# Threshold attention and Fourier mixing on one core: the last 64 queries' scores in four 64x64 tiles of TensorE

## Chip, core and metric

The kernel runs on one core of one Trainium2 chip. The metric is the device time of one execution in microseconds (us). TensorE (PE in the profile) multiplies, VectorE (DVE), ScalarE (ACT) and GpSimd (POOL) work on vectors, and SyncE (SP) issues most of the transfers.

## What is computed

An attention with a threshold, whose output is the input of a block that mixes with a Fourier transform and then applies two dense layers. All of it is fp32.

```python
# q, k, v: (8 batches, 8 heads, 576 positions, 64)
scores = matmul(q, k.T) / 8
thresh = max(scores, axis=-1) - tau               # tau = 0.02
scores = where(scores >= thresh, scores, -1e9)
attn = exp(scores - max(scores)); attn /= sum(attn) + 1e-9
x = matmul(attn, v)            # heads side by side: (8, 576, 512)
mixed = real(fft(fft(x, axis=1), axis=2))
u = x + mixed
un = (u - mean(u)) / sqrt(var(u) + 1e-6)          # over the 512 columns
out = u + maximum(un @ w_ch1, 0) @ w_ch2          # w_ch1: 512x2048, w_ch2: 2048x512
```

## The kernel before, in words

**Pairs and steps.** The attention goes through 32 pairs of heads (8 batches, 4 pairs each), and each pair takes 5 steps, t = 0 to 4, so there are 160 steps i = 5 n + t. A pair's two heads j = 0, 1 lie on the partition halves 0 to 63 and 64 to 127, since a head has 64 columns. Steps 0 to 3 take 128 queries of both heads each: 2 x 128 rows of 576 scores. Step 4 takes the last 64 queries of both heads, which together fill 128 rows.

**Preparation of a pair.** `prep_pair` (L401, in step 3 of the pair before) turns the loaded k and q with VectorE's transposes into kT and qT (L408, L409, L411). kT has 640 columns: the lower half needs the keys in natural order, the upper half has its last 64 keys also in front, so that both heads' last 64 keys end up in the middle of the two rows of weights. `prep_ends` (L416, in step 1) copies on GpSimd the last 64 queries of each head into q_ends, a 128x128 tile whose off-diagonal blocks are zero (L420). `load_v` (L143) loads v of the next pair with two transfers a head: 512 rows and the last 64, whose tile has zeros on the other half.

**Scores** (`scores`, L427). In steps 0 to 3 four matmuls of 64 rows by 128 columns, 288 keys each, one for each half of the keys (c) and head (j), write two PSUM tiles "sc" (L440). In step 4 two matmuls with all 128 rows (L446) multiply the block-diagonal q_ends by kT: each row of the result is one query of one head, with all its 576 scores, in one "sc" tile. There are two "sc" buffers: steps 0 to 3 use both, step 4 uses one.

**Softmax.** VectorE takes the negated maximum of each row (L461 or L520), ScalarE the exponentials (L469, L526) and the threshold (L473, L530), VectorE masks and sums in one instruction (L477, L540), adds 1e-9 and inverts (`inverse`, L385, L388). In the first two batches (steps 0 to 39) `softmax` (L452) does it in one go, and the inverse is spread over columns (`spread_inverse`, L501, L509) and applied later to the values. From the third batch on it comes in three parts with other work between them (`softmax_first`, `_second`, `_third`, L514 to L555), and ScalarE scales the weights themselves (L549). In step 4 there is one row block, so each of these has one instruction, and the last 64 weights are copied next to the others (L504, L554).

**Weights and values.** `weights_in_parts` (L561) transposes the weights of step i - 1 with TensorE: one transpose of the 128 columns that hold both heads' last 64 keys (pe, L587), in the first two batches one of the spread inverse (L590), and four for each head's other 512 keys (pw, L605); step 4 has one pe and four pw. ScalarE copies them out (L593, L597 for step 4's ends; L607, L609). `values_in_parts` (L614) multiplies by v, the two heads in the two column halves of TensorE (L636), and the product waits for ScalarE's copies. PSUM tiles "mm" (pe, pw, pv and the dense layers' ph and po) share four buffers.

**What sets the order.** The program is written out by hand (`manual_schedule`): each engine works through its instructions in the order in which the Python code issues them, and waits only for data and buffers. In the first batch `step` (L1509) issues, for every step, scores, softmax, a column mean of the weights (L360) or filler matmuls (`busy`, L104 to L111) and the transposes of the step before; pieces of the conversion of the dense layers' weights (L296 to L319) go between. In the first batch the scores are sorted by head (L436). The second batch has `second_batch` (L1657); from the third batch on the loop of L1749 puts pieces of the dense layers (L1210, L1400, taken by `fill`, L1489, by a budget of columns) between the parts of the softmax. SyncE's queue carries q, k, v, the dense layers' weights (w<-f, some 1 MB each, issued two loads ahead) and the outputs.

Of the kernel before, what the change touches and what calls it, by code (L numbers as in the profile page):

```python
# [9 lines left out]
FP32 = mybir.dt.float32  # L10
INT32 = mybir.dt.int32
UINT32 = mybir.dt.uint32
ALU = mybir.AluOpType
# [34 lines left out]
def kernel(  # L48
# [94 lines left out]
    def load_v(n):  # L143

        b, p = n // NPAIR, PAIRS[n % NPAIR]
        vt = v_in[n % 2]
        for j in range(2):
            h = 2 * p + (j + p) % 2
            nc.sync.dma_start(
                out=vt[:, j:8:2, :], in_=v[b, h, 0:512, :].rearrange("(t p) d -> p t d", p=128)  # L150
            )
            nc.sync.dma_start(out=vt[64 * j : 64 * j + 64, 8 + j, :], in_=v[b, h, 512:576, :])
# [15 lines left out]


    q_ends = const.tile([128, 128], FP32, name="q_ends")  # L170
    nc.gpsimd.memset(q_ends[:, :], 0.0)
# [211 lines left out]
    def inverse(i, nh):  # L383
        den = sb.tile([128, 2], FP32, tag="den", bufs=3, name="den")
        nc.vector.tensor_reduce(  # L385
            out=den[:, 0:nh], in_=den_eps[i % 3][:, 0:nh, :], axis=AXIS_X, op=ALU.add
        )
        nc.vector.reciprocal(den[:, 0:nh], den[:, 0:nh])  # L388
        return den

    heads = {}
    steps = {}
    xs = {}
# [7 lines left out]
    def prep_pair(n):  # L401

        q_raw, k_raw = loaded.pop(n)
        kT = sb.tile([128, D + S], FP32, tag="kT", name="kT")
        nc.vector.transpose(kT[:, D : D + S], k_raw[:, :])  # L408
        nc.vector.transpose(kT[64:128, 0:D], k_raw[64:128, 512:S])  # L409
        qT = sb.tile([128, S], FP32, tag="qT", bufs=1, name="qT")  # L410
        nc.vector.transpose(qT[:, :], q_raw[:, :])  # L411
        heads[n] = (qT, kT, v_in[n % 2])
        if n + 1 < B * NPAIR and not late:
            load_pair(n + 1)

    def prep_ends(n):  # L416

        for j in range(2):
            hp = slice(64 * j, 64 * j + 64)
            nc.gpsimd.tensor_copy(q_ends[hp, hp], heads[n][0][hp, 512:S])  # L420
# [6 lines left out]
    def scores(i):  # L427
        n, t = divmod(i, NT)
        qT, kT = heads[n][0:2]

        nh = 2 if t < 4 else 1
        sc = [ps.tile([128, 2, 512], FP32, tag="sc", name=f"sc{j}") for j in range(nh)]
        if t < 4:
            order = [(c, j) for c in range(2) for j in range(2)]
            if i < per_batch:
                order.sort(key=lambda cj: cj[1])  # L436
            for c, j in order:
                if True:
                    hp, k0 = slice(64 * j, 64 * j + 64), D * (1 - j)
                    nc.tensor.matmul(  # L440
                        sc[j][:, c, 0:HALF], qT[hp, 128 * t : 128 * t + 128],
                        kT[hp, k0 + HALF * c : k0 + HALF * (c + 1)], start=True, stop=True,
                    )
        else:
            for c in range(2):
                nc.tensor.matmul(  # L446
                    sc[0][:, c, 0:HALF], q_ends[:, :], kT[:, D + HALF * c : D + HALF * (c + 1)],
                    start=True, stop=True,
                )
        steps[i] = (sc, nh)  # L450

    def softmax(i, between=None, meanwhile=None, behind=None):  # L452


        t = i % NT
        sc, nh = steps[i]
        neg = sb.tile([128, 2], FP32, tag="neg", bufs=3, name="neg")
        thr = sb.tile([128, 2], FP32, tag="thr", bufs=3, name="thr")
        e = sb.tile([128, 2 * S], FP32, tag="e", name="e")
        for j in range(nh):  # L460
            nc.vector.tensor_reduce(  # L461
                out=neg[:, j : j + 1], in_=sc[j][:, :, 0:HALF], axis=AXIS_XY, op=ALU.max,
                negate=True,
            )
        if meanwhile is not None:
            meanwhile()
        for j in range(nh):
            ej = e[:, S * j : S * (j + 1)].rearrange("p (c n) -> p c n", c=2)
            nc.scalar.activation(  # L469
                out=ej, in_=sc[j][:, :, 0:HALF], func=ACT.Exp, bias=neg[:, j : j + 1], scale=1.0  # L470
            )
            if j == 0:
                nc.scalar.activation(  # L473
                    out=thr[:, 0:nh], in_=neg[:, 0:nh], func=ACT.Identity,
                    bias=thr_off[:, :], scale=-1.0,
                )
            nc.vector.scalar_tensor_tensor(  # L477
                out=ej, in0=sc[j][:, :, 0:HALF], scalar=thr[:, j : j + 1], in1=ej,
                op0=ALU.is_ge, op1=ALU.mult, accum_out=den_eps[i % 3][:, j, 0:1],
            )  # L480
            if between is not None and j == 0:
                next(between)
        if behind is not None:
            behind()
        den = inverse(i, nh)
        if between is not None:
            for _ in between:
                pass
        if normalized(i // NT):
            nc.vector.tensor_scalar(  # L490
                out=e[:, 0:S], in0=e[:, 0:S], scalar1=den[:, 0:1], scalar2=None, op0=ALU.mult
            )
            if nh == 2:
                nc.scalar.activation(
                    out=e[:, S : 2 * S], in_=e[:, S : 2 * S], func=ACT.Copy, scale=den[:, 1:2]
                )
            steps[i] = (e, None)
        else:
            steps[i] = (e, den[:, 0:nh])

    def spread_inverse(i):  # L501
        e, den = steps[i]
        if i % NT == 4:
            nc.scalar.copy(e[:, S : S + 64], e[:, 512:S])  # L504
        if den is None:
            return
        nh = den.shape[1]
        rec = sb.tile([128, 2 * D], FP32, tag="rec", name="rec")
        nc.scalar.copy(  # L509
            rec[:, :].rearrange("p (j d) -> p j d", j=nh), _repeated(den, 2 * D // nh)  # L510
        )
        steps[i] = (e, rec)

    def softmax_first(i):  # L514
        sc, nh = steps[i]
        neg = sb.tile([128, 2], FP32, tag="neg", bufs=3, name="neg")
        thr = sb.tile([128, 2], FP32, tag="thr", bufs=3, name="thr")
        e = sb.tile([128, 2 * S], FP32, tag="e", name="e")
        for j in range(nh):
            nc.vector.tensor_reduce(  # L520
                out=neg[:, j : j + 1], in_=sc[j][:, :, 0:HALF], axis=AXIS_XY, op=ALU.max,
                negate=True,
            )
        for j in range(nh):
            ej = e[:, S * j : S * (j + 1)].rearrange("p (c n) -> p c n", c=2)
            nc.scalar.activation(  # L526
                out=ej, in_=sc[j][:, :, 0:HALF], func=ACT.Exp, bias=neg[:, j : j + 1], scale=1.0
            )
            if j == 0:
                nc.scalar.activation(  # L530
                    out=thr[:, 0:nh], in_=neg[:, 0:nh], func=ACT.Identity,
                    bias=thr_off[:, :], scale=-1.0,
                )
        steps[i] = (sc, nh, e, thr)

    def softmax_second(i):
        sc, nh, e, thr = steps[i]
        for j in range(nh):
            ej = e[:, S * j : S * (j + 1)].rearrange("p (c n) -> p c n", c=2)
            nc.vector.scalar_tensor_tensor(  # L540
                out=ej, in0=sc[j][:, :, 0:HALF], scalar=thr[:, j : j + 1], in1=ej,
                op0=ALU.is_ge, op1=ALU.mult, accum_out=den_eps[i % 3][:, j, 0:1],
            )
        steps[i] = (nh, e, inverse(i, nh))

    def softmax_third(i):
        nh, e, den = steps[i]
        for j in range(nh):
            nc.scalar.activation(  # L549
                out=e[:, S * j : S * (j + 1)], in_=e[:, S * j : S * (j + 1)], func=ACT.Copy,  # L550
                scale=den[:, j : j + 1],
            )
        if nh == 1:
            nc.scalar.copy(e[:, S : S + 64], e[:, 512:S])  # L554
        steps[i] = (e, None)  # L555
# [5 lines left out]
    def weights_in_parts(i):  # L561
# [25 lines left out]
        nc.tensor.transpose(pe[:, 0, :], e[:, 512:640], ident[:, :])  # L587
# [6 lines left out]
        else:  # L594
            for j in range(2):
                hp = slice(64 * j, 64 * j + 64)
                nc.scalar.copy(ends[hp, 0:kept, q0 : q0 + 64], pe[hp, 0:kept, hp])  # L597
        qs = slice(q0, q0 + (128 if t < 4 else 64))
        for j in range(2 if t < 4 else 1):
# [3 lines left out]
            for c in range(4):  # L603
                c0 = (S + D) * j + 128 * c
# [3 lines left out]
            else:  # L608
                nc.scalar.copy(  # L609
                    e_t[:, :, qs].rearrange("p (j c) q -> p j c q", j=2),  # L610
                    pw[:, :, :].rearrange("p c (j q) -> p j c q", j=2),
# [1298 lines left out]
```

## Time and profile before

| | before |
|---|---|
| median of 3 runs | 1545.87 us (1544.44 to 1548.71) |
| the profiled execution | 1547.94 us |
| its span, first to last instruction | 1546.2 us |
| granted TensorE clock, mean | 0.997 |
| matmul records of TensorE | 9786 |
| step 4 scores (L446) | 128 records of 128x288 columns, 406 ns each |
| steps 0 to 3 scores (L440) | 1024 records of 64 rows, 288 columns, 402 ns or more |

The span is shorter than the execution's time by what lies before the first and after the last instruction. A row of the profile has the line of the kernel, the engine, the operation, out<-in by the program's names and shapes, the number of instructions, and then busy time and mean duration. In the timeline the first two columns are the start and the length of a merged piece, both in us; square brackets tell how long the engine was idle ahead of it and what ended that. A matmul's duration covers its passage through the pipeline, so the cost of one in a row of many is the difference of two starts. Each fp32 matmul leaves two records.

### The profile page before, as it was taken

The page shows a single profiled execution, that of the slowest core. Times are in us where ns is not written, and L with a number is a line of the kernel's source. Part 1 is how long each engine was busy: PE and PEld are TensorE (multiplying, and loading weights), DVE is VectorE, ACT ScalarE, POOL GpSimd, SP SyncE. Part 2 cuts the span into 40 slices and gives each one's busy share as a digit, 9 for nine tenths or more (in the row PEclk, how much of TensorE's full clock was granted, in tenths as well). Part 3 has the DMA queues.
Part 4 walks back from the last instruction along what each step waited for, and adds up shares of the span by engine and source line. Part 5 has one row for each costly group of instructions (what it writes and reads, how often), then busy time and mean ns, then how long its engine had stood idle before and what let it go on. Part 6 is the DMA issues. An engine that isn't in the chain of part 4 may idle for free.

```text
span 1546.2 us, 27021 instructions
## 1 busy us (share of the span) xinstructions
PE 1524.0 (99%) x9786; PEld 1186.0 (77%) x9786; DVE 1063.2 (69%) x2141; ACT 916.4 (59%) x1921; POOL 779.4 (50%) x964
## 2 busy tenths in 40 slices
PE   9999999999999999999999999999999999999999
PEld 5556555556788778887788878887788778989999
DVE  7977676846779466866578566956687657746546
ACT  6875676655666576656775666666665676133131
POOL 3775563034365642546255724554264625647635
PEclk9999999999999999999999999999999999999999
DMA  7423233465956354644455354635464534646655
GB/s 171 130 59 119 78 92 105 139 183 165 280 187 206 92 173 125 186 113 146 146 167 160 120 159 133 199 92 172 120 195 132 160 117 142 220 163 231 234 196 184
DMA packets 248907, 239.31 MB, mean 155 GB/s; under 512 B 197027, under 2 KB 218533, under 8 KB 228678
## 3 DMA queue, kind: packets, MB, share of 16 engines
q1 hardware_dynamic: 246262, 237.28, 50.1%
q8 instruction: 78, 1.28, 0.3%
q10 hardware_dynamic: 2512, 0.30, 0.1%
q14 instruction: 55, 0.45, 0.1%
HBM read 205.93 MB, written 31.46 MB: 154 GB/s over the span
## 4 chain that ended last, share of the span: by engine, by line
PE 91%; DVE 4%; ACT 2%; POOL 1%; DMA 1%; issue 0%; ACTq 0%; DVEq 0%; POOLq 0%
PE ph L1210 25%; PE po L1400 21%; PE pv L636 10%; PE sc L440 10%; PE pw L605 7%; PE po L933 4%; PE ph L909 3%; PE sc L446 2%; PE py L766 2%; PE pe L587 1%; PE pa L783 1%; PE pn L858 1%; PE pa L787 1%; PE pm L360 1%; PE po L1379 1%; DVE neg L461 1%
## 5 line engine op out<-in xcount | busy, mean ns | idle before, releaser
L520 DVE TENSOR_REDUCE neg<-sc 128x1 f32<-128x576 f32 x216 | 154.3, 751 | 117.1 <-PE sc L440 105.5
L526 ACT ACTIVATE e<-sc,neg 128x576 f32<-128x576 f32 x216 | 158.6, 734 | 114.3 <-DVE neg L520 114.3
L1147 DVE TENSOR_TENSOR hs<-ph,hs 128x512 f32<-128x512 f32 (+1 forms) x128 | 105.3, 823 | 167.1 <-PE ph L1210 97.3
L1400 PE MATMUL po<-w,w_all 128*128 128x128 f32 x1728 | 219.4, 276 | 0.0
L1400 PEld LDWEIGHTS po<-w,w_all 128*128 128x128 f32 x1728 | 205.4, 192 | 7.4 <-issue 4.0
L1156 POOL TENSOR_TENSOR w<-hs 128x512 f32<-128x512 f32 x32 | 42.1, 1317 | 312.3 <-ACT hs L1152 249.3
L540 DVE SCALAR_TENSOR_TENSOR e<-sc,thr,e 128x576 f32<-128x576 f32 x216 | 168.4, 812 | 27.2 <-ACT thr L530 27.1
L1210 PE MATMUL ph<-u_t,w 128*128 128x256 f32 x768 | 180.9, 382 | 0.6 <-DMA w<-f 0.6
L607 ACT COPY e_t<-pw 128x512 f32<-128x512 f32 x256 | 148.4, 594 | 44.2 <-PE pw L605 42.7
L440 PE MATMUL sc<-kT,qT 64*128 64x288 f32 x1024 | 168.4, 430 | 5.9 <-DVE e L477 5.5
L605 PE MATMUL pw<-ident,e 128*128 128x128 f32 x1152 | 169.3, 274 | 3.7 <-ACT ends L593 1.9
L549 ACT ACTIVATE e<-e,den 128x576 f32<-128x576 f32 x216 | 157.4, 774 | 2.9 <-DVE den L388 2.2
L1210 PEld LDWEIGHTS ph<-u_t,w 128*128 128x128 f32 x768 | 140.9, 190 | 23.6 <-issue 5.3
L1210 PE MATMUL ph<-w_all,w 128*128 128x256 f32 x672 | 157.1, 382 | 1.1 <-DVE w_all L1132 1.0
L605 PEld LDWEIGHTS pw<-ident,e 128*128 128x128 f32 x1152 | 135.8, 141 | 19.3 <-issue 5.6
L1263 POOL TENSOR_TENSOR w_all<-w_all 128x128 f32<-128x128 f32 (+2 forms) x160 | 121.7, 777 | 44.5 <-DVE w_all L1420 23.4
L1210 PEld LDWEIGHTS ph<-w_all,w 128*128 128x128 f32 x672 | 123.5, 190 | 23.9 <-issue 4.9
L1152 ACT ACTIVATE hs<-hs 128x512 f32<-128x512 f32 (+1 forms) x96 | 74.1, 772 | 113.8 <-DVE hs L1147 113.0
L440 PEld LDWEIGHTS sc<-kT,qT 64*128 64x128 f32 x1024 | 95.1, 186 | 55.4 <-issue 22.9
L1400 PE MATMUL po<-w,hs 128*128 128x128 f32 x912 | 119.8, 278 | 0.0
L1400 PEld LDWEIGHTS po<-w,hs 128*128 128x128 f32 x912 | 109.8, 192 | 9.5 <-issue 8.0
L636 PE MATMUL pv<-e_t,v_in 128*64 128x320 f32 (+1 forms) x512 | 72.1, 423 | 1.5 <-ACT e_t L609 0.8
(227 smaller groups left out, 2910.6 us busy)
## 6 DMA issues: line engine op xcount, KB each, us to landing
w<-f SPq DMA_DIRECT2D x150, 1024.0 KB, 4.9
hs<-in_moe_w_ch_dram SPq DMA_DIRECT2D x23, 512.0 KB, 4.7
q_in<-in_q_dram SPq DMA_DIRECT2D x128, 72.0 KB, 4.1
out_dram<-u SPq DMA_DIRECT2D x36, 256.0 KB, 2.5
k_in<-in_k_dram SPq DMA_DIRECT2D x124, 72.0 KB, 2.4
v_in<-in_v_dram SPq DMA_DIRECT2D x64, 128.0 KB, 5.1
f<-w SPq DMA_DIRECT2D x14, 512.0 KB, 3.3
f<-w SPq DMA_DIRECT2D x7, 1024.0 KB, 4.8
```

The costliest lines, as they stand in the source:

```text
L440: nc.tensor.matmul(sc[j][:, c, 0:HALF], qT[hp, 128 * t : 128 * t + 128], kT[hp, k0 + HALF * c : k0 + HALF * (c + 1)], start=True, stop=True,)
L520: nc.vector.tensor_reduce(out=neg[:, j : j + 1], in_=sc[j][:, :, 0:HALF], axis=AXIS_XY, op=ALU.max, negate=True,)
L526: nc.scalar.activation(out=ej, in_=sc[j][:, :, 0:HALF], func=ACT.Exp, bias=neg[:, j : j + 1], scale=1.0)
L540: nc.vector.scalar_tensor_tensor(out=ej, in0=sc[j][:, :, 0:HALF], scalar=thr[:, j : j + 1], in1=ej, op0=ALU.is_ge, op1=ALU.mult, accum_out ...
L549: nc.scalar.activation(out=e[:, S * j : S * (j + 1)], in_=e[:, S * j : S * (j + 1)], func=ACT.Copy, scale=den[:, j : j + 1],)
L605: nc.tensor.transpose(pw[:, c, :], e[:, c0 : c0 + 128], ident[:, :])
L607: nc.scalar.copy(e_t[:, 4 * j : 4 * j + 4, qs], pw[:, :, :])
L636: nc.tensor.matmul(pv[64 * j : 64 * j + 64, 0:m], vt[:, 2 * c + j, :], e_t[:, 4 * j + c, 0:m] if c < 4 else ends[:, 0, 0:m], start=(c == 0 ...
L1147: nc.vector.tensor_tensor(out=to, in0=bank, in1=to if other is None else other, op=ALU.add)
L1210: nc.tensor.matmul(bank[:, 256 * q : 256 * q + 256].rearrange("p (two n) -> p two n", two=2), left[:, 256 * c + 128 * q : 256 * c + 128 * ...
L1263: return lambda: eng.tensor_tensor(out=to, in0=to, in1=other, op=ALU.add)
L1400: nc.tensor.matmul(to, lefts[m][j][:, s], right_[:, 128 * s : 128 * (s + 1)], start=jn in (0, 4) and s == 0, stop=s == 3, skip_group_check ...
```

## The change

In step 4 the four products (c, j) of half of the keys and one head become four matmuls of 64 rows by 64 columns, 288 keys each, which write one "sc" tile: head j in bank j, half c of the keys on the partition half c. A query's scores are then spread over two partitions, p and p + 64, with 288 each. So:

- q_ends holds the 64 queries of each head on its own partition half, 128x64, and one GpSimd copy fills it for two before.
- The maximum is taken over 288 scores on each partition, the halves are exchanged by two minima over one element (64 partitions each), and a third minimum joins them (`maxima`, `exchange`). The sums are exchanged in the same way ahead of the inverse (den_ends).
- Exponentials, masks and the late scaling have one instruction for each head with 288 columns in place of one with 576. In step 4 `softmax` issues both exponentials ahead of the masks. The copy of the last 64 weights goes.
- The middle 64 keys (256 to 319) take the place of the last 64 as the part that both heads share in one transpose. So kT has another order and 672 columns, made by two transposes of 320 columns and two of 32 on 64 partitions; v is loaded in three transfers a head for two; steps 0 to 3 have matmuls of 256 and 320 keys, in opposite order for the two heads, and their 576 scores lie in a row across the two banks.
- Step 4's ends are copied out in four pieces of 32 partitions in place of two of 64, and in the first two batches its spread inverse in a piece of its own.

The number of matmul instructions rises from 64 to 128 for step 4's scores and stays the same elsewhere; VectorE's instructions rise by 257, ScalarE's by 96, GpSimd's fall by 33, and 64 transfers are added.

```diff
     def load_v(n):
...
-            nc.sync.dma_start(
-                out=vt[:, j:8:2, :], in_=v[b, h, 0:512, :].rearrange("(t p) d -> p t d", p=128)
-            )
-            nc.sync.dma_start(out=vt[64 * j : 64 * j + 64, 8 + j, :], in_=v[b, h, 512:576, :])
+            for first, k0 in ((0, 320), (2, 0)):
+                nc.sync.dma_start(
+                    out=vt[:, first + j : 8 : 4, :],
+                    in_=v[b, h, k0 : k0 + 256, :].rearrange("(t p) d -> p t d", p=128),
+                )
+            nc.sync.dma_start(out=vt[64 * j : 64 * j + 64, 8 + j, :], in_=v[b, h, 256:320, :])
...
-    def inverse(i, nh):
+    def inverse(i):
         den = sb.tile([128, 2], FP32, tag="den", bufs=3, name="den")
...
+        parts = den_eps[i % 3]
+        if i % NT == 4:
+            parts = den_ends
+            exchange(parts[:, :, 2], parts[:, :, 0:1])
+        nc.vector.tensor_reduce(out=den[:, :], in_=parts[:, :, :], axis=AXIS_X, op=ALU.add)
+        nc.vector.reciprocal(den[:, :], den[:, :])
...
-        kT = sb.tile([128, D + S], FP32, tag="kT", name="kT")
-        nc.vector.transpose(kT[:, D : D + S], k_raw[:, :])
-        nc.vector.transpose(kT[64:128, 0:D], k_raw[64:128, 512:S])
+        kT = sb.tile([128, S + 96], FP32, tag="kT", name="kT")
+        nc.vector.transpose(kT[:, 0:320], k_raw[:, 256:S])
+        nc.vector.transpose(kT[:, 352:672], k_raw[:, 0:320])
+        for j, k0 in ((0, 288), (1, 256)):
+            hp = slice(64 * j, 64 * j + 64)
+            nc.vector.transpose(kT[hp, 320:352], k_raw[hp, k0 : k0 + 32])
...
     def prep_ends(n):
...
-        for j in range(2):
-            hp = slice(64 * j, 64 * j + 64)
-            nc.gpsimd.tensor_copy(q_ends[hp, hp], heads[n][0][hp, 512:S])
+        nc.gpsimd.tensor_copy(q_ends[:, :], heads[n][0][:, 512:S])
...
     def scores(i):
...
+        order = [(c, j) for c in range(2) for j in range(2)]
+        if i < per_batch and t < 4:
+            order.sort(key=lambda cj: cj[1])
+        for c, j in order:
+            hp = slice(64 * j, 64 * j + 64)
+            if t < 4:
+                k0, k1 = ((64, 320), (352, 672), (0, 320), (352, 608))[2 * j + c]
+                to = sc[j][:, c, 512 - (k1 - k0) : 512] if c == 0 else sc[j][:, c, 0 : k1 - k0]
+                left = qT[hp, 128 * t : 128 * t + 128]
+            else:
+                k0, k1 = ((64, 352), (352, 640), (32, 320), (320, 608))[2 * j + c]
+                to, left = sc[0][64 * c : 64 * c + 64, j, 0:HALF], q_ends[hp, :]
+            nc.tensor.matmul(
+                to, left, kT[hp, k0:k1], start=True, stop=True, skip_group_check=t == 4
+            )
...
-            for c in range(2):
-                nc.tensor.matmul(
-                    sc[0][:, c, 0:HALF], q_ends[:, :], kT[:, D + HALF * c : D + HALF * (c + 1)],
-                    start=True, stop=True,
...
+    def maxima(i):
...
+        nc.vector.tensor_reduce(
+            out=own[:, :, 0], in_=both, axis=AXIS_X, op=ALU.max, negate=True
+        )
+        exchange(own[:, :, 1], own[:, :, 0:1])
+        nc.vector.tensor_reduce(out=neg[:, :], in_=own[:, :, :], axis=AXIS_X, op=ALU.min)
+        return neg
+
+    def exchange(out_, in_):
+
+        for half in range(2):
+            a, b = 64 * half, 64 - 64 * half
+            nc.vector.tensor_reduce(
+                out=out_[a : a + 64], in_=in_[b : b + 64], axis=AXIS_X, op=ALU.min
+            )
...
     def softmax(i, between=None, meanwhile=None, behind=None):
...
+        if i % NT == 4:
+            exponentials(i, e, neg, thr, 0)
+        for j in range(2):
+            if i % NT < 4:
+                exponentials(i, e, neg, thr, j)
+            elif j == 0:
+                exponentials(i, e, neg, thr, 1)
+            masked(i, e, thr, j)
...
     def spread_inverse(i):
         e, den = steps[i]
-        if i % NT == 4:
-            nc.scalar.copy(e[:, S : S + 64], e[:, 512:S])
...
             for j in range(2):
-                hp = slice(64 * j, 64 * j + 64)
-                nc.scalar.copy(ends[hp, 0:kept, q0 : q0 + 64], pe[hp, 0:kept, hp])
+                for half in range(2):
+                    p0 = 64 * j + 32 * (1 - half)
+                    nc.scalar.copy(
+                        ends[p0 : p0 + 32, 0, q0 : q0 + 64],
+                        pe[32 * j : 32 * j + 32, 0, 64 * half : 64 * half + 64],
+                    )
+            if kept == 2:
+                nc.scalar.copy(ends[:, 1, q0 : q0 + 64], pe[:, 1, 0:64])
```

## The prediction

> **What bounds the kernel now.** I read the page first: totals, slices, chain of the work that ended last.
>
> ```profile
> span 1546.2 us, 27021 instructions
> ...
> PE 1524.0 (99%) x9786; PEld 1186.0 (77%) x9786; DVE 1063.2 (69%) x2141; ACT 916.4 (59%) x1921; POOL 779.4 (50%) x964
> ...
> DVE  7977676846779466866578566956687657746546
> ...
> PE 91%; DVE 4%; ACT 2%; POOL 1%; DMA 1%; issue 0%; ACTq 0%; DVEq 0%; POOLq 0%
> ```
>
> TensorE is the bound; VectorE is nearly full only at the left. The windows view separates two regimes (PE, PEld, DVE, ACT, POOL busy; then the clock):
>
> ```profile
> 60.00:80.00 20.00, 19.17 (x95) 11.21 (x93) 18.21 (x40) 16.90 (x38) 12.51 (x15) 1.00 0.44 110
> 80.00:100.00 20.00, 18.03 (x86) 10.46 (x86) 16.20 (x39) 15.85 (x35) 14.67 (x17) 0.91 0.41 98
> 600.00:800.00 200.00, 199.48 (x1412) 163.68 (x1411) 136.74 (x285) 131.87 (x278) 101.04 (x126) 1.00 0.48 144
> ```
>
> Until about 205 us TensorE stands still now and then while VectorE is 90% busy; from there it hardly stops. So a saving on TensorE counts after 205 us, and a longer softmax counts before it. Next the timeline of TensorE around one step 4 (L446) and one step 0 (L440) of a late pair, and one value product (L636):
>
> ```profile
> 754.47 1.13 PE L446 MATMUL sc<-kT,q_ends 128*128 128x288 f32 x4
> 755.44 1.89 PE L1210 MATMUL ph<-u_t,w 128*128 128x256 f32 x8
> 757.16 0.27 PE L587 MATMUL pe<-ident,e 128*128 128x128 f32 x1
> ...
> 761.70 1.24 PE L440 MATMUL sc<-kT,qT 64*128 64x288 f32 x8
> 762.87 0.48 PE L1210 MATMUL ph<-t_room,w 128*128 128x256 f32 x1
> ...
> 768.79 1.24 PE L440 MATMUL sc<-kT,qT 64*128 64x288 f32 x8
> 769.97 2.37 PE L636 MATMUL pv<-e_t,v_in 128*64 128x320 f32 x16
> 772.17 0.71 PE L636 MATMUL pv<-ends,v_in 128*64 128x320 f32 x4
> 772.81 1.56 PE L1210 MATMUL ph<-w_all,w 128*128 128x256 f32 x6
> ```
>
> Differences of starts, not ends, tell what TensorE pays, since matmuls are pipelined. Each fp32 matmul leaves two records. L446: 4 records in 0.97 us, 242 ns each. L440: 8 records of the same width in 1.17 us: two run at a time (64 rows each). L636: 20 records of 320 columns in 2.84 us: two at a time again (64 columns each).
>
> **The skill's rules.** The Trainium skill, "TensorEngine Tiling (Array Packing)", section Key Properties, says that different tiles load weights and multiply in parallel, and that a change of the tiling mode drains TensorE. Both show here, with the price that I use: the L440 group takes 1171 ns instead of 4 x 242 = 970, and the record ahead of it lasts some 94 ns more than its usual 109 to 216. So 94 on entry, about 104 behind the first pair (second weights not hidden), about 90 on exit. In L636, whose weights are 64 columns, the middle term is 52. Four tiles of 64x64 at once no trace here shows; the skill, "TensorE: Matmul & The Clock Gate", Part 3, gives a packed span of one matmul plus about 4 ns per further tile. Rows and columns each overlap here (starts 6 to 7 ns apart), so I go by it, with 7 ns.
>
> **The change part by part.** There are 32 pairs, one step 4 in each.
>
> TensorE. Before: 970 ns. After: entry 94, first pass 242 + 52, second 242 + 90, spread of four tiles 21: 741. It saves 0.23 us a pair. Bounds: overlap without any drain, 485, saves 0.49; only two tiles at a time, 94 + 4x242 + 52 + 90 = 1204, costs 0.23; no overlap, 94 + 8x242 + 142 = 2172, costs 1.20. The transposes keep their number. Steps 0 to 3 now have 256 + 320 columns for 288 + 288, in opposite order for the two heads: the same 576 a head, cost 0 if each half runs as its own stream. In step 2 of the first batch one head started between the other's records and did not disturb its 242 ns spacing, so I take 0.
>
> VectorE. A reduce of two pairs of numbers is 157 ns, the next starts 190 ns later. Maxima: two exchanges and a final minimum, +3x0.19 = 0.57. Masking: 576 columns take 812 ns, transposes of 576 and 64 columns 774 and 242, thus 1.04 ns a column; halves are 512, plus 82 for the accumulator: 2x594 against 894, +0.29. Sums: two exchanges, +0.38. Layout of k in prep_pair: 2 x 508 + 2 x 209 against 774 + 242, +0.42. In all 1.66 us a pair, 53 us: 1063 becomes about 1116.
>
> ScalarE. Exponentials 2x490 against 734, +0.25. Late pairs: scaling 2x531 against 775, +0.29; the 64-column copy goes, -0.24; four 32-row copies for two at 208, +0.42. Some 0.7 us a pair, 21 us. In the first 8 pairs the copies of the ends are five for two, 1040 against 522.
>
> GpSimd: one copy for two, and a memset less: nothing, it is 50% busy and in the chain with 1%. SyncE: two more v issues a pair, the same bytes; four q issues took 1.96 us, so +1 us on a queue that also carries the weight loads (w<-f). TensorE waited 0.6 us in all for these; they are issued two loads ahead and v a pair ahead. Cost 0, at most 1 us if that lead is gone.
>
> Where is the cover? **After 205 us** the next scores start at least 1.6 us after the mask of step 4 is done (2.4 from the third batch on), and there the transposes 1.8 to 4.8 us after its last ScalarE step. The mask comes 0.57 + 0.29 = 0.9 later, the weights about 1.3. (In the second batch the transposes stand 0.2 us behind the 64-column copy, which goes.) So the 0.23 is kept: steps 34 to 159, 26 of them, and steps 14 and 24, where the next scores start 1.2 and 1.3 us after the mask (tight). 28 x 0.229 = **-6.4 us**.
>
> **Before 205 us** steps 4, 9, 19 and 29 have no cover: the next step's second score tile needs the buffer (two "sc") that step 4's mask frees. Step 9:
>
> ```profile
> 59.52 1.14 PE L446 MATMUL sc<-kT,q_ends 128*128 128x288 f32 x4
> 61.33 0.74 DVE L461 TENSOR_REDUCE neg<-sc 128x1 f32<-128x576 f32 x1
> 62.11 0.74 ACT L469 ACTIVATE e<-sc,neg 128x576 f32<-128x576 f32 x1 [0.41 <-DVE neg L461]
> 62.75 0.28 ACT L473 ACTIVATE thr<-neg,thr_off 128x1 f32<-128x1 f32 x1
> 63.26 0.81 DVE L477 SCALAR_TENSOR_TENSOR e<-sc,thr,e 128x576 f32<-128x576 f32 x1
> ```
>
> The scores of step 10 start at 63.39 while this mask runs to 64.07, and their group takes 1.91 us instead of 1.17. VectorE never rests here, so it hands on 0.42 + 0.57 + 0.29 = 1.28 us, and behind the waiting matmul stand the eight column-mean matmuls (L360). Step 29 likewise: 1.28. Step 19: VectorE had waited 0.28 for TensorE and then 0.99 for the threshold; 0.73 for the mask, and 0.52 for the copies of the ends, for which a value product waits (0.80 at 124.78): 1.25. Step 4: VectorE had 0.82 us of rest ahead of step 5's maxima; about 0.8 is left. Start: the first scores wait for prep_pair, 0.42. Together **+5.0 us**; bounds 0 (rest elsewhere takes it up) and about 11 (see the clock).
>
> Sum: -6.4 + 5.0 = **-1.4 us**. The profiled execution took 1547.94 (span 1546.2 and 1.7 around it), so it would be 1546.5; it lies 2.1 above the median of 1545.87, from which I predict 1544.5.
>
> **Rivals.** 0.3%, 4.6 us, is about what a measurement of this kernel can tell from no change.
> A. As above: 1544.5, chance 0.43.
> B. The early delays are taken up. For it: VectorE idles 9% even at 60 to 80 us, and much early TensorE work is filler (L111). Against: the chain goes through steps 4, 9 and 19. All 32 pairs gain, or 28 and a little is paid: -6 to -7.3, about 1539.3. Chance 0.25.
> C. Slower: only two of the four tiles run at once. The place is L446's successor; it decides once the third record starts about 240 ns after the first instead of 14. For it: no trace here shows rows and columns split together. +0.23 x 28 = 6.4, + 5.0: 1557.3. Chance 0.15.
> D. The unequal widths run in lockstep: each pass of a pair takes 269 ns (as L636's 320 columns) instead of 242, +0.11 us in 128 steps, +13.7 - 1.4: 1558.2. Against: the stream above. 0.08.
> E. The clock: after a stop of 2.1 us at 78.9 us the records from 81.7 to about 85 come at twice their spacing, and the granted clock of that window is 0.91. Early stops of 1.1 to 1.3 us (12, 39, 99, 181 us) that grow by 1.3 reach that length; three episodes of some 2 us each give -1.4 + 6: 1550.5. 0.07.
> F. No overlap at all: 28 x 1.2 + 5 = +39: 1585. 0.02.
>
> **Numbers.** Faster by over 0.3%: B, 0.25. Within: A, 0.43. Slower: C to F, 0.32. The range runs from B's 1539 to C's 1557.5; most of D, F and the outer parts of B and C lie outside. A alone: 1541.5 to 1549.
>
> **What would show it.** The group of 64x64 scores: four records within 25 ns, some 0.65 us to the next record, the one ahead 94 ns longer. TensorE records 128 more. Groups of steps 0 to 3 still 1171 ns (D: 1280). VectorE near 1116, ScalarE near 937 busy. Up to 205 us: the work is there about 5 us later than before, with score groups after steps 4, 9, 19, 29 over a microsecond longer; after 205 us, 6 us are won back at an even pace. The forecast is wrong if the third record starts late, if steps 34 on bring new stops on TensorE, or if the early part is not later.

## The result, and the profile after

| | before | after |
|---|---|---|
| median | 1545.2 us, 4 runs (1544.44 to 1548.71) | 1558.95 us, 4 runs (1557.35 to 1563.56) |
| ratio | | 1.0093, 95% interval 1.0067 to 1.0118 |
| the profiled execution | 1547.94 us, clock 0.997 | 1557.35 us, clock 0.999 |

The change costs 13.7 us. The forecast was 1544.5, no change; the result lies even above the upper end of its range. The page of after, with the lines that answer to those of before:

```profile
span 1555.6 us, 27727 instructions
...
PE 1520.4 (98%) x9914; PEld 1182.5 (76%) x9914; DVE 1097.6 (71%) x2430; ACT 930.0 (60%) x2017; POOL 767.9 (49%) x931
...
DVE  7987677846879566866688566956687667846546
...
PE 79%; DVE 11%; ACT 5%; DMA 2%; issue 1%; SPq 1%; POOL 0%; ACTq 0%; DVEq 0%
```

TensorE is busy 3.6 us less, in a span that is 9.4 us longer: it stands still more. The chain says behind whom: VectorE's share of it went from 4% to 11%, ScalarE's from 2% to 5%, although VectorE is still only 71% busy. The windows view of after, for the stretches shown of before:

```profile
60.00:80.00 20.00, 19.48 (x100) 11.07 (x96) 18.49 (x46) 16.49 (x40) 11.76 (x14) 1.00 0.49 123
80.00:100.00 20.00, 18.05 (x92) 10.10 (x90) 16.62 (x46) 16.09 (x35) 14.06 (x16) 0.91 0.42 97
600.00:800.00 200.00, 198.49 (x1408) 162.80 (x1407) 141.54 (x324) 132.94 (x289) 96.13 (x120) 1.00 0.49 147
```

From 600 to 800 us TensorE has lost 0.99 us of its 199.48, while VectorE's work rose from 136.74 to 141.54. That is a stage for which the forecast had promised a gain. The waits of TensorE say on what (total us, times, longest), first before:

```profile
PE sc L440 <- DVE e L477: 5.5, 7, 1.2
PE ph L1210 <- DVE hs L1147: 2.1, 5, 0.8
...
PE pv L636 <- ACT e_t L609: 0.8, 1, 0.8
...
PE pw L605 <- DVE w_all L1420: 0.2, 1, 0.2
```

and after:

```profile
PE sc L453 <- DVE e L510: 8.5, 11, 1.2
PE ph L1243 <- DVE hs L1180: 3.1, 5, 1.6
PE pw L639 <- DVE w_all L1453: 2.4, 5, 0.6
PE pv L669 <- ACT e_t L643: 2.1, 3, 1.2
...
PE py L799 <- ACT y_o L804: 1.7, 4, 0.4
...
PE po L1433 <- ACT w_all L1445: 1.4, 4, 0.4
```

The first row is the wait that the forecast had in view: score tiles held by step 4's mask. The fourth is a value product that waits for ScalarE's copy of step 4's own weights. The others are banks of the dense layers and inputs of the Fourier transform (py), which have nothing to do with step 4 except that their work stands behind it on VectorE and ScalarE.

**Where the time went.** I laid the same TensorE records of both traces side by side. After is later by 1.3 us at step 40 and by 8.65 us at the end. The granted clock of before was 0.91 from 100 to 120 us and 0.97 from 160 to 220 us, that of after 1.00, so this pair of profiles understates the early part; for its size see the experiments. The later 7.3 us come in jumps: 0.56 to 0.80 us ahead of pw in the step 4 of the first pair of a batch (steps 64, 104, 124, 144), 0.36 to 0.39 more ahead of py just behind it, 0.52 at po in steps 80, 120 and 140, 0.86 at ph in step 54, and 1.1 at the scores of step 41 and the value products behind them, still an effect of step 39. Another 0.46 is a longer wait for one weight load (w<-f) near the end. That wait lasts between nothing and 1.0 us in the fourteen traces, and its cause was not looked for.

**One such place, step 124.** The timeline of before (start, length, both in us):

```profile
1008.87 0.74 DVE L520 TENSOR_REDUCE neg<-sc 128x1 f32<-128x576 f32 x1
...
1009.54 0.67 DVE L1420 TENSOR_TENSOR w_all<-w_all,po 128x512 f32<-128x512 f32 x1
...
1010.50 0.33 PE L587 MATMUL pe<-ident,e 128*128 128x128 f32 x1
...
1010.66 0.60 PE L605 MATMUL pw<-ident,e 128*128 128x128 f32 x4
```

The same place after:

```profile
1014.91 0.75 DVE L483 TENSOR_REDUCE own<-sc 128x2 f32<-128x576 f32 x1
...
1015.70 0.31 DVE L494 TENSOR_REDUCE own<-own 64x2 f32<-64x2 f32 x2
...
1015.91 0.33 PE L612 MATMUL pe<-ident,e 128*128 128x128 f32 x1
1016.04 0.16 DVE L487 TENSOR_REDUCE neg<-own 128x2 f32<-128x4 f32 x1
1016.12 0.69 DVE L1453 TENSOR_TENSOR w_all<-w_all,po 128x512 f32<-128x512 f32 x1
...
1016.87 0.66 PE L639 MATMUL pw<-ident,e 128*128 128x128 f32 x4 [0.63 <-DVE w_all L1453]
...
1017.29 0.60 ACT L804 COPY y_o<-py 48x256 f32<-48x256 f32 x1
...
1017.94 0.66 PE L799 MATMUL py<-dim_c,f 128*128 128x65 f32 x4 [0.41 <-ACT y_o L804]
```

The transposes pw need one of the four "mm" banks, and the bank comes free when VectorE has added the dense layer's product po (w_all). Before, this addition starts 0.67 us after the maximum and ends 0.29 us ahead of pe; pw follows pe at 0.16. After, the two exchanges and the third minimum stand between, and it starts 1.21 us after the maximum: +0.54. VectorE also comes to the maximum only 1.00 us ahead of pe instead of 1.63. Together the bank is free 0.90 us after pe has started, and pw follows pe at 0.96 instead of 0.16: TensorE stands for 0.80 us. ScalarE gets its exponentials late too, the copy y_o stands behind the second, and py waits for that.

**TensorE's side.** The timeline of TensorE around a late step 4, after:

```profile
757.29 1.89 PE L1243 MATMUL ph<-w_all,w 128*128 128x256 f32 x8
759.12 0.72 PE L453 MATMUL sc<-kT,q_ends 64*64 64x288 f32 x8
759.76 1.99 PE L1243 MATMUL ph<-u_t,w 128*128 128x256 f32 x8
761.59 0.27 PE L612 MATMUL pe<-ident,e 128*128 128x128 f32 x1
```

The eight records start at 0, 7, 13, 20 and 293, 300, 307, 313 ns; the next work starts 646 ns after the first, and the record ahead lasts 94 ns longer: 740 ns, as predicted. What I had missed stands one line on. The eight ph records behind the group take 1.83 us (759.76 to 761.59); before they took 1.72 (755.44 to 757.16). The second of them starts 104 ns late. The trace of before shows the same behind L440 (its second record of po comes at 213 ns for 112). So a pair gains 0.231 - 0.104 = 0.127 us.

**An early step 4** (step 9, whose rows of before stand in the prediction):

```profile
61.73 0.74 DVE L483 TENSOR_REDUCE own<-sc 128x2 f32<-128x576 f32 x1
...
62.85 0.16 DVE L487 TENSOR_REDUCE neg<-own 128x2 f32<-128x4 f32 x1
...
64.66 0.52 DVE L510 SCALAR_TENSOR_TENSOR e<-sc,thr,e 128x288 f32<-128x288 f32 x1
...
65.23 1.02 PE L453 MATMUL sc<-kT,qT 64*128 64x320 f32 x3 [0.52 <-DVE e L510]
```

The mask ends at 65.18; before it ended at 64.07. The second head's scores of step 10 wait for it until 65.23.

### The profile page after: what moved, and what is told of

The parts are those of the page before. It is cut to its first block, busy times and chain, and to the rows that moved or that the text cites. A ratio compares the mean times of both kernels' runs of the same rounds, so it can differ in the third digit from the quotient of the medians.

```text
span 1555.6 us, 27727 instructions
## 1 busy us (share of the span) xinstructions
PE 1520.4 (98%) x9914; PEld 1182.5 (76%) x9914; DVE 1097.6 (71%) x2430; ACT 930.0 (60%) x2017; POOL 767.9 (49%) x931
## 4 chain that ended last, share of the span: by engine, by line
PE 79%; DVE 11%; ACT 5%; DMA 2%; issue 1%; SPq 1%; POOL 0%; ACTq 0%; DVEq 0%
PE ph L1243 24%; PE po L1433 19%; PE pv L669 9%; PE sc L453 9%; PE pw L639 6%; PE po L966 3%; DVE e L510 2%; ACT e L499 2%; PE py L799 2%; PE ph L942 1%; DVE neg L475 1%; PE pa L816 1%; PE pa L820 1%; PE pm L359 1%; DMA hs<-in_moe_w_ch_dram 1%
## 5 line engine op out<-in xcount | busy, mean ns | idle before, releaser
L499 ACT ACTIVATE e<-sc,neg 128x576 f32<-128x576 f32 (+1 forms) x320 | 220.1, 688 | 159.8 <-DVE neg L475 120.7
L475 DVE TENSOR_REDUCE neg<-sc 128x1 f32<-128x576 f32 x256 | 182.0, 751 | 112.4 <-PE sc L453 112.4
L510 DVE SCALAR_TENSOR_TENSOR e<-sc,thr,e 128x576 f32<-128x576 f32 (+1 forms) x320 | 229.0, 753 | 40.1 <-ACT thr L504 22.2
L1180 DVE TENSOR_TENSOR hs<-ph,hs 128x512 f32<-128x512 f32 (+1 forms) x128 | 105.0, 820 | 153.1 <-PE ph L1243 84.2
L453 PE MATMUL sc<-kT,qT 64*128 64x256 f32 (+1 forms) x1024 | 170.4, 429 | 9.6 <-DVE e L510 8.5
L578 ACT ACTIVATE e<-e,den 128x576 f32<-128x576 f32 (+1 forms) x240 | 161.8, 726 | 5.8 <-DVE den L393 5.6
L453 PEld LDWEIGHTS sc<-kT,qT 64*128 64x128 f32 x1024 | 110.2, 186 | 53.0 <-issue 25.3
```

The source lines that it names most:

```text
L453: nc.tensor.matmul(to, left, kT[hp, k0:k1], start=True, stop=True, skip_group_check=t == 4)
L475: nc.vector.tensor_reduce(out=neg[:, j : j + 1], in_=sc[j], axis=AXIS_X, op=ALU.max, negate=True)
L499: nc.scalar.activation(out=weights_of(i, e, j), in_=steps[i][j], func=ACT.Exp, bias=neg[:, j : j + 1], scale=1.0,)
L510: nc.vector.scalar_tensor_tensor(out=ej, in0=steps[i][j], scalar=thr[:, j : j + 1], in1=ej, op0=ALU.is_ge, op1=ALU.mult, accum_out=(den_en ...
L578: nc.scalar.activation(out=ej, in_=ej, func=ACT.Copy, scale=den[:, j : j + 1])
L1180: nc.vector.tensor_tensor(out=to, in0=bank, in1=to if other is None else other, op=ALU.add)
```

## The experiments

Ratios are to before, timed on the same chip, with 95% intervals; before was at 1544.45 in the runs of the first four kernels, 1545.14 in those of the next four, and 1545.0 in those of the last four. After is taken at 1558.95, +13.75 us. It has four runs, and its interval reaches from +10 to +18 us, so a difference against it is no surer than that.

The times also go with the granted clock, which varied from run to run. Of before, 26 runs at 1.00 took 1543.3 to 1543.9 us (mean of each group), 48 at 0.999 took 1544.6 to 1544.9, and 10 at 0.997 took 1547.3 to 1548.3. After had two runs at 0.999 (1557.4) and two at 0.995 and 0.996 (1563.6 and 1560.4). At an equal clock of 0.999 it is therefore 12.6 us slower than before. Where the clock changes a reading, it is said below.

**1. scores_only: before, with only step 4's scores in four tiles.** q_ends is 128x64. A row of step 4's softmax has the same half of the keys of both heads in it.

```diff
-                nc.tensor.matmul(
-                    sc[0][:, c, 0:HALF], q_ends[:, :], kT[:, D + HALF * c : D + HALF * (c + 1)],
-                    start=True, stop=True,
-                )
+                for j in range(2):
+                    hp = slice(64 * j, 64 * j + 64)
+                    nc.tensor.matmul(
+                        sc[0][64 * c : 64 * c + 64, j, 0:HALF], q_ends[hp, :],
+                        kT[hp, D + HALF * c : D + HALF * (c + 1)], start=True, stop=True,
+                        skip_group_check=True,
+                    )
```

> The kernel before with step 4's scores alone changed: four 64x64 matmuls in place of two 128x128. Everything behind them is as before, so a row of step 4's softmax takes half of the keys of both heads for its own; this leaves out the right pairing of scores and rows. It isolates TensorE. As in the prediction (0.23 us saved a pair): 6 to 7 us faster than before. Theory Q (what the two traces show: 0.23 saved, then 0.10 given back in the second record behind the group, so 0.13 a pair): 3 to 4 us faster.

Measured: 1541.7, ratio 0.9983 (0.9977 to 0.999), -2.75 us. In 31 of the 32 pairs the second record behind the group is 101 to 105 ns late, in one 56. 32 x 0.127 = 4.06, so part of the gain is lost, most of it early, where TensorE waits anyway: from step 40 on the trace wins 2.7 us of the 3.05 that 24 pairs would give. The TensorE part alone is a gain, and a smaller one than I had.

**2. layout: the key order, v and the unequal widths of steps 0 to 3; step 4 as before,** with a block-diagonal q_full and matmuls of 256 and 320 keys. Against after:

```diff
+    def split(i):
+        return False
...
+        if t == 4 and not split(i):
+            order = []
+            nc.tensor.matmul(
+                sc[0][:, 0, 256:512], q_full[:, :], kT[:, 64:320], start=True, stop=True
+            )
+            nc.tensor.matmul(
+                sc[0][:, 1, 0:320], q_full[:, :], kT[:, 352:672], start=True, stop=True
+            )
```

> The changed kernel's order of keys (kT by four transposes, v in three transfers, 256 and 320 columns in steps 0 to 3), with the softmax and the scores of step 4 as before: one block-diagonal tile, two matmuls of 256 and 320 columns, no exchange. Theory Q: the loss lies in step 4's longer softmax, so this is 0 to 2 us slower than before (0.42 us more VectorE a pair, which counts only in the first batches). Rival L (layout and transfers are the cause): 8 us or more slower.

Measured: 1546.72, 1.0014 (1.0007 to 1.0021), +2.3. A little more than expected. In the traces 0.8 us of it come from step 40 on, where the forecast had put nothing.

**3 and 4. early and late: layout, with the split step 4 in the first two batches only, or from the third on only.**

```diff
     def split(i):
-        return False
+        return i % NT == 4 and i < 40
```

(late has i >= 40. The rival E of these two expectations is not the prediction's rival E.)

> The layout kernel with the split step 4 in the first two batches only (steps 0 to 39). Theory Q (step 4's longer softmax holds up TensorE in every batch): 4 to 7 us slower than before. Rival E (the loss is all in the early part, as the prediction had it, where the score buffer is waited for, and the late stops are an accident of one profile): 10 to 13 us slower.

> The layout kernel with the split step 4 from the third batch on (steps 40 to 159). Theory Q: from step 40 to the end the changed kernel's trace falls back by 7.3 us, so 7 to 9 us slower than before. Rival E: the late pairs gain 24 x 0.13 = 3 us, so 1 to 3 us faster than the layout kernel.

Measured: early 1552.62, 1.005 (1.0038 to 1.0062), +5.9 over layout. late 1552.01, 1.0047 (1.0035 to 1.0059), +5.3 over layout. 2.3 + 5.9 + 5.3 = 13.5 of the 13.75. early was more than I expected, and about 3 us of it is the clock: its five runs were granted 0.997 or 0.998, those of layout 0.999 or 1.00 in 17 of 22. layout's trace has a clock of 1.00 in every stretch up to 220 us; early's has 0.91 from 0 to 20 us and 0.83 from 80 to 90, and there its records fall behind by 1.7 and 1.5 us. Before has such stretches in its own profile (0.83 from 80 to 90 and from 100 to 110 us), so it is not shown that the change brings them on. Without them early costs some 2.7 over layout, 1.7 of it behind steps 34 and 39: a value product waits 0.53 us for ScalarE's copies, which are five pieces for two there, and step 41's scores wait for step 40's mask. The parts then make 10.3, against 12.6 for after at an equal clock; some 2 us are not accounted for.

late settles where the forecast fell: from step 40 on the split costs 5.3 us where a gain was promised. The traces of layout and late, both at a clock of 1.00, account for it: late comes to be 4.9 us behind; 24 pairs gain 0.127 each (-3.05), so 8.0 us of stops stand against that. Fourteen single stops over 0.3 us make 7.2 of them: 2.7 ahead of pw in steps 64, 104, 124 and 144, 1.2 ahead of py behind it, 1.6 at po in steps 80, 120 and 140, and 1.8 at four other places.

**5. no_exchange: after, without the exchanges of maxima and sums and without the third minimum.** Each half row is normalized by itself.

```diff
-            exchange(parts[:, :, 2], parts[:, :, 0:1])
...
-        exchange(own[:, :, 1], own[:, :, 0:1])
-        nc.vector.tensor_reduce(out=neg[:, :], in_=own[:, :, :], axis=AXIS_X, op=ALU.min)
-        return neg
+        return own[:, :, 0]
```

**6. no_max_exchange: only the second part of that diff;** the sums are still joined.

> The changed kernel without both exchanges and the third minimum: each partition takes the maximum and the sum of its own 288 scores for the whole. This leaves out that the two halves of a query are joined. It takes 0.95 us of the 1.66 us that a pair adds to VectorE. Theory Q (the stops come from what is queued on VectorE behind step 4's longer softmax): 4 to 8 us slower than before, against 13.7 for the changed kernel. Rival S (the pieces on ScalarE do it): 11 us or more.

> The changed kernel without the exchange of the maxima and the third minimum (0.57 us of VectorE a pair); sums are still exchanged. This leaves out that the halves' maxima are joined. Theory Q, with the maxima on the path to the mask and the sums behind it: most of what the run without both wins, so 6 to 10 us slower than before. If the sums count as much as the maxima: 9 to 11.

Measured: no_exchange 1545.28, 1.0006 (0.9996 to 1.0016); no_max_exchange 1547.52, 1.0014 (1.0007 to 1.0021). Both gave back far more than I expected. Five small instructions a pair are nearly the whole loss: joining the sums costs 2.2 us, joining the maxima 11.4. At an equal clock of 0.999 the latter is 9.9 (after 1557.4, no_max_exchange 1547.5). It is three instructions that take VectorE 0.54 us in step 124, some 17 us in 32 pairs, on an engine that is 71% busy. The waits tell which stops go. In no_max_exchange:

```profile
PE py L797 <- ACT y_o L802: 1.5, 4, 0.4
...
PE pw L637 <- DVE w_all L1451: 0.4, 1, 0.4
```

The 2.4 us ahead of pw are down to 0.4, and po's 1.4 behind ScalarE's w_all are gone. But py still waits 1.5 us of its 1.7 for y_o, in no_exchange too: that stop belongs to the other added work, not to the joins. Step 124 of no_max_exchange:

```profile
1008.12 0.75 DVE L483 TENSOR_REDUCE own<-sc 128x2 f32<-128x576 f32 x1
...
1008.79 0.68 DVE L1451 TENSOR_TENSOR w_all<-w_all,po 128x512 f32<-128x512 f32 x1
...
1009.12 0.33 PE L610 MATMUL pe<-ident,e 128*128 128x128 f32 x1
...
1009.52 0.66 PE L637 MATMUL pw<-ident,e 128*128 128x128 f32 x4
```

The addition follows the maximum at 0.67 again, and pw follows pe at 0.40: 0.56 of the 0.80 us are gone. The other 0.24 stay, because the maximum is still only 1.00 us ahead of pe. So the delay that VectorE brings along comes from the other added work.

**7. one_piece: after, with one exponential, mask and scaling of 576 columns in step 4;** the first head's maximum, threshold and sum serve both.

```diff
-            steps[i] = [sc[0][:, j, 0:HALF] for j in range(2)]
+            steps[i] = [sc[0][:, :, 0:HALF]]
...
-            return e[:, HALF * j : HALF * (j + 1)]
+            return e[:, 0:S].rearrange("p (c n) -> p c n", c=2)
```

> The changed kernel with one exponential, one mask and one late scaling of 576 columns in step 4, as before, in place of two of 288; exchanges stay. This takes the first head's maximum, threshold and sum for both heads. It takes 0.29 us of VectorE and 0.25 (late pairs 0.54) us of ScalarE a pair. Theory Q: 10 to 13 us slower than before. Rival S: 5 to 8 us slower.

Measured: 1554.12, 1.0065 (1.0051 to 1.0078), +9.0: 4.8 of the 13.75 go with the pieces, more than I expected. With the joins gone the pieces cost almost nothing: no_exchange is at +0.1, where scores_only (-2.75) and layout (+2.3) make -0.5. So the costs don't add one by one. Each takes from the same slack, and counts once that is used up. The Trainium skill, "Perfetto Trace Analysis", section Optimizing Scalar/DVE Operations, says that breaking up instructions may let work complete sooner where ScalarE and VectorE are not saturated but cause bubbles elsewhere. Here they are not (71% and 60%), and two pieces are slower than one.

**8. rest: late, but the first pair of each batch as before.**

```diff
     def split(i):
-        return i % NT == 4 and i >= 40
+        return i % NT == 4 and i >= 40 and i // NT % NPAIR > 0
```

> The layout kernel with the split step 4 from the third batch on, but not in the first pair of a batch, where the mixing's products stand between. Theory Q: the stops in those first pairs (six batches, 0.9 to 1.2 us each) go and 18 x 0.13 = 2.3 us is kept, so 1 to 3 us faster than the late kernel, 4 to 6 us slower than before. Rival (the stops are spread evenly over the pairs): as the late kernel less a quarter of its 5.3 us over the layout kernel, 6 us or more slower than before.

Measured: 1547.98, 1.0017 (1.0009 to 1.0024), +2.8. That is 0.6 over layout: in these 18 pairs a gain of 18 x 0.127 = 2.3 is eaten by 2.9 of stops. The six first pairs cost the rest of late, 7.56 - 2.84 = 4.7, or 0.8 each. Leaving them out was also the attempt at a version that beats before; since layout alone costs 2.3, as much as the 18 pairs could win, it can't.

**9 and 10. three_ahead and three_behind: before, with three small minima in step 4,** between its maximum and its exponential, or behind its mask. In three_ahead the exponential reads the last one's result, which equals the maximum.

```diff
+    def three(neg):
+        for a in (0, 64):
+            nc.vector.tensor_reduce(
+                out=neg[a : a + 64, 1:2], in_=neg[a : a + 64, 0:1], axis=AXIS_X, op=ALU.min
+            )
+        nc.vector.tensor_reduce(out=joined[:, :], in_=neg[:, :], axis=AXIS_X, op=ALU.min)
+        return joined
...
+        if t == 4:
+            neg = three(neg)
```

> The kernel before with three small minima on VectorE between step 4's maximum and its exponential (two over one element on 64 partitions, one over two on 128), as many as the changed kernel's exchange has; the result is the same maximum. It adds the disputed 0.57 us a pair alone, with no split. Theory P (it is their place ahead of the exponential, which everything else that VectorE and ScalarE release for TensorE stands behind): 8 to 12 us slower than before, as the run without them won 11. If the cost came with the split of the tiles: 0 to 3 us slower.

> The same three minima in the kernel before, issued behind step 4's mask, where nothing waits for them. Theory P: 0 to 2 us slower. Rival O (VectorE's time as such counts, wherever it is spent): as much as with the minima ahead, 8 to 12 us.

Measured: three_ahead 1550.74, 1.0032 (1.0021 to 1.0042), +5.7; three_behind 1545.64, 1.0003 (0.9994 to 1.0011), +0.6. The same instructions cost 5.7 us in one place and nothing that can be told from noise in the other, with nothing else of the change in the kernel. In before there is more slack than in after, so it is half of the 11.4 and less than I expected. TensorE's waits of three_ahead:

```profile
PE ph L1224 <- DVE hs L1161: 2.6, 5, 1.3
...
PE py L780 <- ACT y_o L785: 0.8, 3, 0.3
```

Two of the stops of after are there; before has no row for y_o there, and 0.8 as the longest for hs.

**11. exchange_behind: after, with the joining of the maxima behind the masks.** Its result isn't used, so each half row takes its exponentials with its own maximum.

```diff
+        return own[:, :, 0]
+
+    joined = const.tile([128, 2], FP32, name="joined")
+
+    def join():
         exchange(own[:, :, 1], own[:, :, 0:1])
-        nc.vector.tensor_reduce(out=neg[:, :], in_=own[:, :, :], axis=AXIS_X, op=ALU.min)
-        return neg
+        nc.vector.tensor_reduce(out=joined[:, :], in_=own[:, :, :], axis=AXIS_X, op=ALU.min)
```

> The changed kernel with the exchange of the maxima and the third minimum issued behind the masks and used by nobody: each half takes its own maximum (the halves are not joined), all instructions are there. Theory P: 2 to 5 us slower than before, as without them. Rival O: 11 to 14 us, as the changed kernel.

Measured: 1551.38, 1.0034 (1.0021 to 1.0047), +6.4. Between no_max_exchange (+2.4) and after (+13.75): of the 11.4 us, 4 remain with the instructions behind the masks, 7.4 are their place ahead of the exponentials. In this kernel, with its other added work, VectorE's time has a price of its own, more than I expected, but the place is the larger part (at an equal clock of 0.999, 3.4 and 6.5).

**12. two_ops: after, with the three reduces replaced by two minima of two operands,** which gives the same result.

```diff
-        exchange(own[:, :, 1], own[:, :, 0:1])
-        nc.vector.tensor_reduce(out=neg[:, :], in_=own[:, :, :], axis=AXIS_X, op=ALU.min)
+        for a, b in ((0, 64), (64, 0)):
+            nc.vector.tensor_tensor(
+                out=neg[a : a + 64, :], in0=own[a : a + 64, :, 0], in1=own[b : b + 64, :, 0],
+                op=ALU.min,
+            )
```

> The changed kernel with the maxima joined by two instructions in place of three: a minimum of the own and of the other half's, one for each half of the partitions. The result is the changed kernel's. If the price goes with the number of small instructions on the path: 13.7 - 11.4/3, 9 to 11 us slower than before. If it is a threshold that two of them stay below: 5 us or less.

Measured: 1565.73, 1.0129 (1.0114 to 1.0144), +20.7: one instruction less, and 7 us more than after. About 5 of them are left at an equal clock (0.996: 1565.5 in two runs, after 1560.4 in one). The durations (least, median, longest, in ns) of its 64 minima:

```profile
L487 DVE TENSOR_TENSOR neg<-own x64: 153/156/1193, 32.8 to 1320.5; 64x2 f32<-64x2 f32 x64
```

and step 124 of two_ops:

```profile
1019.46 1.26 POOL L1227 TENSOR_TENSOR w_all<-hs,w_all 128x512 f32<-128x512 f32 x1 [1.34 <-issue]
1019.61 1.30 DVE L487 TENSOR_TENSOR neg<-own 64x2 f32<-64x2 f32 x2
...
1020.94 0.69 DVE L1456 TENSOR_TENSOR w_all<-w_all,po 128x512 f32<-128x512 f32 x1
...
1021.68 0.66 PE L642 MATMUL pw<-ident,e 128*128 128x128 f32 x4 [1.53 <-DVE w_all L1456]
```

So the run does not answer what it was to ask, whether the number of instructions counts: these are of another kind. The first minimum starts beside a running addition of GpSimd and is done only when that ends; the bank comes free later by as much, and pw waits for 1.53 us. This agrees, in the other direction, with the reading that TensorE pays for what stands between the maximum and the addition.

## Why the prediction was wrong, point by point

- **"After 205 us", with "So the 0.23 is kept": this step failed.** It was checked only for step 4's own consumers, the next scores and its own transposes. From step 40 on those had room; behind steps 34 and 39, which were counted as covered too, they had not (1.7 us). And VectorE and ScalarE work in order, and what stands in their queues behind step 4's maximum and exponentials was not checked: the additions that free the dense layers' banks (L1453, L1180), the copies y_o (L804) and w_all (L1445). There the room in step 124 was under half a microsecond (the bank was free 0.29 us ahead of pe, and pw is due 0.16 after it). From step 40 on, 24 pairs were to bring -5.5; they cost 5.3 (late). New stops from step 34 on were the prediction's own sign of being wrong, and they came.
- **0.23 us a pair: mis-sized.** The group itself is right to 1 ns (740 for 741), and 64x64 tiles do run four at a time. The term "exit" ended one record too soon: the second record behind the group is 104 ns later. Worth 0.127 a pair, and 2.75 us in all (scores_only) instead of 6.4.
- **Early steps, +5.0: right in mechanism, near in size partly by luck.** The mask of step 9 ends 1.1 us later, and the next score tile waits for it. early is 8.2 over before (5.9 over layout), inside the bounds of 0 and 11, but about 3 of that is the clock. The 5 that are left contain 1.7 behind steps 34 and 39, where the forecast had none.
- **Layout, GpSimd, SyncE: no large stop.** Layout costs 2.3 in all, near the 2.1 of its 0.42 us in five early places. That is in part luck, since 0.8 of it comes from step 40 on. The one wait for a weight load grew by 0.46 us in after, within the bound of 1. Groups of steps 0 to 3 still take 1171 ns, so rival D fell. Rival C fell with the third record at 14 ns. Rival B fell: the early delays were not taken up. Rivals C and D gave nearly the right time (1557.3 and 1558.2) by mechanisms that did not happen. Rival E, the clock, is not excluded: early's times hold some 3 us of it, but no run shows that the longer stops bring it on.
- **Busy times:** records of TensorE +128 as predicted; VectorE 1098 where I had 1116, of which 6 are that a small reduce is busy for 149 to 159 ns and I had counted 190, the distance of two starts (the rest was not traced); ScalarE 930 where I had 937.

By cause, the 13.7 us are: -2.75 four tiles, +2.3 layout, +0.6 the pieces without joins (no_exchange less the two before), +2.2 joining the sums, +11.4 joining the maxima. The last three depend on the order in which they are added, since they share one slack, and the 11.4 holds the lower clock of two of after's runs (9.9 at an equal clock). Not settled is what share each piece of the other added work has in the 0.63 us that VectorE brings along to step 124.

## What to carry to other kernels

When an instruction is added to an engine that is far from full, ask what stands behind it in that engine's queue, and which of those frees a bank or feeds a copy that TensorE needs next: the room that counts is the smallest of all of these, not that of the instruction's own consumers. Price small instructions by their place: three minima of 0.15 us in each of 32 pairs cost 5.7 us ahead of the exponential, and nothing that could be told from noise behind the mask. And compare times at the same granted clock when a few us matter. For a tiled group of matmuls, compare the starts of the next two records, not of the next one, with their usual distance.

## What the runs showed of the hardware that was not expected

- A VectorE instruction with two operands in SBUF waited for a running GpSimd instruction, small as it was: 64x2 elements took 156 ns in the median, and 18 of the 64 took 229 to 1193, each ending 13 to 20 ns after a TENSOR_TENSOR of GpSimd (two_ops). Reduces with one operand never did. In after 26 of these 64 ran wholly inside such an instruction (least, median, longest):

```profile
L494 DVE TENSOR_REDUCE own<-own x64: 148/149/152, 32.7 to 1311.5; 64x2 f32<-64x2 f32 x64
```

  The Trainium skill, "SBUF — State Buffer", section SBUF: two separate sides, states this rule for a VectorE instruction with two inputs in SBUF against a GpSimd one that reads SBUF: an exclusive lock on ports that the two engines share, for the whole instruction. These runs agree.
- Behind a group in 64x64 tiles, TensorE is late once more at the second record of the next work: by 101 to 105 ns in 31 of the 32 pairs of scores_only, by 56 in the other.
